# One operation and one transpose for the statistics' rows of two token tiles

## The chip, the core and the metric

The kernel runs on one core of a Trainium2 chip. The core has five engines that run at the same time and wait for each other through semaphores: PE (TensorE, matrix products), DVE (VectorE), ACT (ScalarE), POOL (GpSimd) and SP (which here only issues loads and stores). Each engine takes its instructions strictly in the order in which the program gives them. Operands lie in SBUF; PE writes to PSUM, which has eight banks here, each holding one 128x512 tile of fp32.

The metric is the device time of one execution in microseconds (us). For the kernel before the change the median of three runs is 441.87 us (440.46 to 442.1). The profiled execution, from which every duration below is taken, took 440.71 us; the span between its first and last instruction is 439.0 us.

## The reference

The block is a linear-attention block followed by a token-mixing MLP, both with a layer norm modulated by vectors that come from `c`. Sizes: 2048 tokens (S), 448 channels (D), 16 heads of 28, 1792 hidden features.

```python
x = A_x
mod = (_silu(c) @ w_mod).reshape(c.shape[0], 6, 1, -1)
sa, ca, ga, sb, cb, gb = (mod[:, 0], mod[:, 1], mod[:, 2], mod[:, 3], mod[:, 4], mod[:, 5])
h = _layernorm(x, axis=-1) * (1 + ca) + sa
x = x + ga * _A_ref(h, A_wqkv, A_wo)
h = _layernorm(x, axis=-1) * (1 + cb) + sb
x = x + gb * _B_ref(h, B_w1, B_b1, B_w2, B_b2)

def _A_ref(x, wqkv, wo):
    qkv = (x @ wqkv).reshape(B, S, 3, H, Dh).transpose(2, 0, 3, 1, 4)
    phi = lambda t: jnp.where(t > 0, t + 1, jnp.exp(t)) + 1e-6
    pq, pk = phi(q), phi(k)
    kv = jnp.einsum("bhsd,bhse->bhde", pk, v)
    z = jnp.einsum("bhsd->bhd", pk)
    num = jnp.einsum("bhqd,bhde->bhqe", pq, kv)
    den = jnp.einsum("bhqd,bhd->bhq", pq, z)[..., None] + 1e-6
    return (num / den).transpose(0, 2, 1, 3).reshape(B, S, D) @ wo
```

The change concerns the first layer norm alone: the mean and the standard deviation of each token over its 448 channels.

## The kernel before, in words

The tokens are cut into 16 tiles of 128. Every product is made with three single-pass products of a number cut into a high part (rounded) and a low part (the rest): high by high, high by low, low by high. In names, `hh` and `hl` are the high and low parts of a transposed token tile, `pkh` and `pkl` those of phi(k), `xh` and `xl` those of the normalized tile, `wh` and `wl` those of the weights.

The work runs in three stages. The first, up to about 101 us, makes phi(k) of all token tiles and sums the outer product of phi(k) with the normalized tiles in four PSUM banks (`cacc`). The second, to about 234 us, makes the attention output, the second layer norm and the first products of the MLP. The third makes the rest of the MLP. The change lies in the first stage only.

In the first stage the layer norm is not applied ahead of the projection. `project` (L428) multiplies the raw token tile by the weights in ten matmuls into a bank `kp`; `close` (L432) adds one more matmul, which multiplies four rows of statistics by four rows that were summed from the weights; and `a_exp` (L438) applies the reciprocal standard deviation as the scale of the exponential. The four rows of one tile are the mean and the standard deviation, each in a high and a low part. They come about in this way:

- `a_stats_dve` (L368): VectorE makes mean and variance of a tile (`bn_stats` into `st`, `bn_aggr` into `mv`), adds epsilon (`ve`), and GpSimd raises that to the powers 0.5 and -0.5 (`a_pow`, L348), so that `mv` holds mean, standard deviation and its reciprocal. Tiles 0 to 3 are done on ScalarE instead, tiles 4 and 5 as a pair, and from tile 6 on one tile at a time (`a_stats`).
- `a_rows` (L386): VectorE writes mean and standard deviation into columns of a 128x128 tile `rowst`, first the high parts (a CAST, which rounds), then the low parts (a subtraction, L391). `RING` such tiles are used in turn.
- `a_transpose` (L395): PE turns `rowst` into a PSUM bank `rw`.
- `a_copy` (L401): ScalarE copies 34 rows of the bank into a free corner of the tile's `hl`, where `close` reads them.

The order of the work is written out by hand: each engine's queue is the order of the calls in the code. After a start-up part, steps t = 4 to 15 of a loop (L628) do in this order: `project` of tile t+1, `close` of tile t, `a_transpose` of tile t+1, the outer product `a_outer` of tile t-4 (11 matmuls), from step 10 on also a projection to q (`a_q`, bank `qp`), then the rows of tile t+2, the statistics of tile t+3, ScalarE's copy of the transposed rows of tile t+1, `a_exp` of tile t, and the cuts of the tiles t+3, t-1 and t-2 into parts.

PSUM banks come from one pool of eight (`bank`). Four of them are `cacc` for the whole stage, so `kp`, `rw`, `qp` and a few others take turns in the other four: the first matmul into a bank waits until the reader of what stood there is done.

Of the kernel before, what the change touches and what calls it, by code (L numbers as in the profile page):

```python
# [14 lines left out]
P = 128  # L15
S, D, F = 2048, 448, 1792
NT = S // P
# [33 lines left out]
def block_kernel(ctx: ExitStack, tc: tile.TileContext, x, xt, wqkv, wo, w1, b1, w2, b2, c, wmod, wfirst, out):  # L51
# [276 lines left out]
            done["split"] += 1  # L328


    heads, mv, xn = {}, {}, {}
    junk = slot("junk")

    def b_square(src, nm, acc, name):
# [15 lines left out]
    def a_stats_act(ts):  # L350
        n = len(ts)
        g, ve = a_group(ts)
        sm = small.tile([P, n, 3], F32, name=f"as{ts[0]}", tag=f"as{n}")

        def one(i):
            t, s3 = ts[i], sm[:, i, :]
            nc.scalar.activation(junk, X[t], AF.Identity, accum_out=s3[:, 0:1])
            nc.scalar.activation(s3[:, 1:2], s3[:, 0:1], AF.Copy, scale=-1.0 / D)
            b_square(X[t], s3[:, 1:2], s3[:, 2:3], f"s{t}")

        def end():
# [3 lines left out]
            a_pow(g, ve)  # L365
        return one, end

    def a_stats_dve(ts):  # L368
        g, ve = a_group(ts)

        def one(i):
            b6 = small.tile([P, 6], F32, name=f"st{ts[i]}", tag="st")
            nc.vector.bn_stats(b6, X[ts[i]])
            nc.vector.bn_aggr(mv[ts[i]][:, 0:2], b6)

        def end():
            nc.vector.tensor_scalar_add(ve, g[:, :, 1:2].to_broadcast([P, len(ts), 2]), EPS)  # L377
            a_pow(g, ve)
        return one, end

    def a_stats(t):
        one, end = a_stats_dve((t,))
        one(0)
        end()

    def a_rows(t):  # L386
        r = rowst[t % RING]
        pair = mv[t][:, 0:2]
        nc.vector.tensor_copy(r[:, 64:].rearrange("p (b c) -> p b c", b=2)[:, :, 0:2],
                              pair.unsqueeze(1).to_broadcast([P, 2, 2]))  # L390
        nc.vector.tensor_sub(r[:, 66:68], pair, r[:, 64:66].bitcast(F32))  # L391

    tps = {}

    def a_transpose(t0, n=1):  # L395
        ps = bank(f"rw{t0}")
        for i in range(n):
            tps[t0 + i] = ps[:, i * P:(i + 1) * P]
            nc.tensor.transpose(tps[t0 + i][:ROWS], rowst[(t0 + i) % RING][:, :ROWS].bitcast(F32), ident)

    def a_copy(t):  # L401
        nc.scalar.activation(heads[t][1][64:ROWS, 384:], tps.pop(t)[64:ROWS], AF.Copy)

    def a_split_high(t):
        heads[t] = (slot(f"hh{t}", 512, F32R), slot(f"hl{t}", 512, F32R))
# [115 lines left out]
    def a_outer(t):  # L521
        if not cacc:
            cacc.extend(bank(f"cacc{ch}") for ch in range(4))
        xh, xl = xss.pop(t)
        kh, kl = pks.pop(t)
        for ch in range(4):
            s = slice(ch * P, (ch + 1) * P)
            todo = [(xh, kh), (xh, kl)] + ([(xl, kh)] if ch < 3 else [])
            for i, (a, b) in enumerate(todo):
                nc.tensor.matmul(cacc[ch][:, :D], a[:, s], b, start=(t == 0 and i == 0),  # L530
                                 stop=(t == NT - 1 and i == len(todo) - 1))

    pc = bank("col1")
    for k in range(2):
# [26 lines left out]
    col_out(0, pc)  # L561
    for ch in range(4):
        row_part(1, ch)
    a_rows(0)
    a_rows(1)
    project(3, 1, "kp")
    a_transpose(0, 2)
    row_bias(1)
    a_split(4)
    a_norm(0)  # L570
    dve45, end45 = a_stats_dve((4, 5))
    dve45(0)
    act23, end23 = a_stats_act((2, 3))
    act23(0)
    act23(1)
    end23()
    a_copy(0)
    a_copy(1)
    row_out(1)
    a_rows(2)  # L580
    a_rows(3)
    a_high(0)
    load_xt(9)
    load_x(9)
# [4 lines left out]
    a_split(5)  # L589
    a_low(0)  # L590
    kps = [close(t, 1) for t in (0, 1)]
    a_transpose(2, 2)
    project(5, 1, "kp")
    a_exp(0, kps[0])
    a_pk(0, kps[0])
    dve45(1)
    end45()
    a_copy(2)
    a_copy(3)
# [3 lines left out]
    a_pk_parts(0)  # L603
    a_outer(0)
    a_pk(1, kps[1])
    a_rows(4)
    a_rows(5)
    a_transpose(4, 2)
    a_exp(2, kps[2])
    a_split_high(6)  # L610
    a_pk(2, kps[2])
# [16 lines left out]
    for t in range(4, NT):  # L628
        if 5 < t < NT - 1:
            project(t + 1, 1, "kp")  # L630
        kp = close(t, 1) if t > 4 else kps[4]
        if 4 < t < NT - 1:
            a_transpose(t + 1)
        if t == 9:
            row_sum(0)
            row_bias(0)
        if t > 4:
            a_outer(t - KV_LAG)
        if t in Q_EARLY:
            a_q(Q_EARLY[t])  # L640
        if t == 12:
            mp = mod_sum2(2)
        if 4 < t < NT - 2:
            a_rows(t + 2)
        if 5 <= t < 9:
            w_low(0, t - 5)
            row_part(0, t - 5)
        if 7 < t + 3 < NT:
            a_stats(t + 3)
        a_phi_q(t in Q_EARLY)  # L650
        if 4 < t < NT - 1:
            a_copy(t + 1)
        a_exp(t, kp)
        if t + 3 < NT:
            a_split_high(t + 3)
# [2 lines left out]
        for i in highs[:1]:  # L658
            a_norm(i)
            a_high(i)  # L660
        a_pk(t, kp)
        if t + 3 < NT:
            a_split_low(t + 3)
        for i in highs[1:]:
# [622 lines left out]
```

## Time and profile before

| | busy | share of the span |
|---|---|---|
| span of the profiled execution | 439.0 us (the execution: 440.71 us) | |
| PE matmul | 433.3 us | 99% |
| DVE | 364.0 us | 83% |
| ACT | 279.4 us | 64% |
| POOL | 118.2 us | 27% |

The part that the change touches, by stretches of the same profile (us of busy time in each):

| stretch, us | PE | DVE | ACT | POOL |
|---|---|---|---|---|
| 20 to 37 (17.0) | 16.13 | 15.50 | 15.65 | 6.60 |
| 37 to 57 (20.0) | 19.95 | 19.52 | 18.61 | 11.92 |
| 57 to 101 (44.0) | 44.00 | 34.97 | 29.05 | 13.37 |
| 101 to 234 (133.0) | 133.00 | 114.67 | 99.36 | 54.46 |

A row of the timeline view, which is used most below, has the start in us from the span's start, the duration in us, the engine, the line of the code, the operation, `out<-in` by the tiles' names, shapes, a count of merged instructions, and in brackets the idle time of the engine before it with what ended it. Matmuls overlap: one is shown for about 0.36 us, but the next one starts about 0.20 us after it. Time that PE loses is therefore read from the distance of two starts, not from the idle time alone.

### The profile page before, as it was taken

To read this page: it belongs to the slowest core of one execution; us is meant where nothing else is said; L and a number is where in the kernel's file an instruction comes from. 1 tells how busy PE (TensorE), PEld (TensorE's weight loads), DVE (VectorE), ACT (ScalarE), POOL (GpSimd) and SP (SyncE) were. 2 spreads that over 40 slices of the span, in tenths; PEclk is the share of its full clock that TensorE was granted. 3 is DMA by queue.
4 is the path that set the end of the run, shared out by engine and by line. 5 is a ranking of instruction groups with operands and counts; after the bars stand their busy time and mean duration, and the time that the engine had idled before them with its cause. 6 is when DMAs were issued, how large, how long until landed. Compare 5 with 4: busy or idle time off the path is not lost.

```text
span 439.0 us, 7315 instructions
## 1 busy us (share of the span) xinstructions
PE 433.3 (99%) x2383; PEld 401.3 (91%) x2383; DVE 364.0 (83%) x822; ACT 279.4 (64%) x598; POOL 118.2 (27%) x200
## 2 busy tenths in 40 slices
PE   8999999999999999999999999999999999999996
PEld 7878899999899999999999999999999999999996
DVE  3989998689889999995579785829799988898894
ACT  3899877657676698885765263627555555655550
POOL 3137554300004567783300000010112231132010
PEclk9999999999999999999999999999999999999999
DMA  7997999545410025534616661579379987985430
GB/s 244 385 311 162 220 227 246 95 140 187 127 30 1 24 50 135 105 74 96 193 61 199 204 189 45 145 206 234 59 182 229 193 183 156 225 171 125 85 52 32
DMA packets 64085, 66.17 MB, mean 151 GB/s; under 512 B 4976, under 2 KB 55600, under 8 KB 64048
## 3 DMA queue, kind: packets, MB, share of 16 engines
q1 hardware_dynamic: 55120, 51.17, 38.3%
q0 software_dynamic: 8928, 14.55, 21.0%
q8 instruction: 18, 0.29, 0.3%
q14 instruction: 19, 0.16, 0.1%
HBM read 46.11 MB, written 7.34 MB: 122 GB/s over the span
## 4 chain that ended last, share of the span: by engine, by line
PE 96%; DVE 1%; ACT 1%; issue 0%; ACTq 0%
PE y L1077 19%; PE up L860 10%; PE up L861 10%; PE up L862 10%; PE y L1078 9%; PE op L810 8%; PE cacc L530 8%; PE qp L426 7%; PE kp L426 6%; PE tq L785 1%; PE col L218 1%; PE warm L181 1%; PE qp L433 1%; PE kvb L741 1%; PE rowb L283 1%; PE wp L877 1%
## 5 line engine op out<-in xcount | busy, mean ns | idle before, releaser
L860 PE MATMUL up<-h2h,ph 128*128 128x448 f32 x224 | 81.3, 363 | 0.0
L862 PE MATMUL up<-h2h,pl 128*128 128x448 f32 x224 | 81.1, 362 | 0.0
L861 PE MATMUL up<-h2l,ph 128*128 128x448 f32 x224 | 80.9, 361 | 0.0
L1032 POOL DMA_DIRECT2D a<-a x16 | 14.2, 963 | 139.4 <-DMA pr<-in_B_w_dram 75.3
L862 PEld LDWEIGHTS up<-h2h,pl 128*128 128x128 f32 x224 | 42.0, 188 | 3.1
L861 PEld LDWEIGHTS up<-h2l,ph 128*128 128x128 f32 x224 | 41.9, 187 | 3.1 <-DVE h2l L857 0.3
L860 PEld LDWEIGHTS up<-h2h,ph 128*128 128x128 f32 x224 | 42.0, 188 | 2.5
L83 DVE TENSOR_TENSOR pl<-pr,ph 128x512 fp32r<-128x512 f32 x46 | 30.8, 688 | 4.1 <-ACT ph L82 3.3
L1083 ACT ACTIVATE cc<-y 128x448 f32<-128x448 f32 x24 | 13.0, 546 | 26.8 <-PE y L1078 26.8
L82 ACT ACTIVATE ph<-pr 128x512 fp32r<-128x512 f32 x46 | 27.6, 624 | 0.8 <-PE up L862 0.5
L996 DVE TENSOR_TENSOR u<-u,mod 128x448 f32<-128x448 f32 x14 | 8.7, 623 | 21.6 <-ACT u L995 21.4
L530 PE MATMUL cacc<-pkh,xh 128*128 128x448 f32 x64 | 24.4, 382 | 0.3 <-ACT pkh L504 0.3
L810 PE MATMUL op<-wph,pth 128*128 128x448 f32 x64 | 24.5, 383 | 0.0
L995 ACT ACTIVATE u<-up,b1c 128x448 f32<-128x448 f32 x14 | 8.8, 625 | 24.1 <-PE up L862 23.5
L530 PE MATMUL cacc<-pkl,xh 128*128 128x448 f32 x64 | 23.3, 364 | 0.2 <-DVE pkl L506 0.2
L426 PE MATMUL kp<-wh,hh 128*128 128x448 f32 x64 | 23.2, 373 | 0.2 <-ACT wh L256 0.2
L426 PE MATMUL qp<-wh,hh 128*128 128x448 f32 x64 | 23.3, 364 | 0.0
L810 PE MATMUL op<-wpl,pth 128*128 128x448 f32 x64 | 23.1, 362 | 0.0
L1097 POOL DMA_DIRECT2D out_dram<-yt x14 | 12.5, 893 | 39.1 <-DVE yt L1088 29.7
L767 POOL TENSOR_SCALAR den<-den 128x16 f32<-128x16 f32 x16 | 8.8, 549 | 47.7 <-DVE den L764 47.7
L348 POOL TENSOR_TENSOR mv<-ve,roots 128x2 f32<-128x2 f32 (+1 forms) x13 | 12.5, 960 | 22.4 <-DVE ve L377 21.6
L1038 DVE TENSOR_TENSOR a<-a,s 128x512 f32<-128x512 f32 (+1 forms) x32 | 18.5, 619 | 0.0
(238 smaller groups left out, 1382.7 us busy)
## 6 DMA issues: line engine op xcount, KB each, us to landing
pr<-in_B_w_dram SPq DMA_DIRECT2D x56, 256.0 KB, 3.3
a<-in_B_w_dram SPq DMA_DIRECT2D x32, 256.0 KB, 4.8
a<-in_B_w_dram SPq DMA_DIRECT2D x32, 192.0 KB, 4.6
xt<-in_xt_dram SPq DMA_DIRECT2D x16, 256.0 KB, 4.9
x<-in_A_x_dram SPq DMA_DIRECT2D x16, 224.0 KB, 4.8
wm<-in_B_wmod_dram SPq DMA_DIRECT2D x16, 196.0 KB, 4.8
out_dram<-x SPq DMA_DIRECT2D x14, 224.0 KB, 2.2
out_dram<-yt POOLq DMA_DIRECT2D x14, 224.0 KB, 6.3
```

The source lines that it names most:

```text
L82: nc.scalar.activation(hi, full, AF.Copy)
L83: nc.vector.tensor_sub(lo, full, hi.bitcast(F32))
L426: nc.tensor.matmul(pps[t, j][:, :D], a[:, ch * P:(ch + 1) * P], w, start=first, stop=False)
L530: nc.tensor.matmul(cacc[ch][:, :D], a[:, s], b, start=(t == 0 and i == 0), stop=(t == NT - 1 and i == len(todo) - 1))
L810: nc.tensor.matmul(opb[t][:, :D], a, b, start=(n == 0), stop=(n == len(todo) - 1))
L860: nc.tensor.matmul(ps[:, :D], hi[:, sl], mh, start=first, stop=False)
L861: nc.tensor.matmul(ps[:, :D], hi[:, sl], ml, start=False, stop=False)
L862: nc.tensor.matmul(ps[:, :D], lo[:, sl], mh, start=False, stop=last)
L1032: nc.gpsimd.dma_start(w, a, accum_op=ALU.add)
L1038: nc.vector.tensor_tensor(w, raw2[q, a][i], raw2[q, b][i], op=op)
L1077: nc.tensor.matmul(ps[:, :D], h[:, s], w, start=opens and r == 0, stop=False, skip_group_check=True)
L1078: nc.tensor.matmul(ps[:, :HD], l[:, s], wh, start=False, stop=closes and r == PAIRS - 1, skip_group_check=True)
```

## The change

The rows of two neighbouring tiles are made together. `rowst` now has room for two tiles, 64 columns each, and the ring has three of them instead of six. One CAST writes the high parts of both tiles, one subtraction the low parts of both, one transpose turns both, and the two copies read rows 0 to 33 and 64 to 97 of the same bank. From tile 6 on the statistics are finished for pairs too: one `ve` and one power for two tiles.

With that the calls move. In the loop, odd steps t = 5 to 13 transpose the tiles t+1 and t+2, behind the outer product of the step and no longer ahead of it, and ScalarE copies both at that step. The rows of the pair (t+2, t+3) are made at even steps t = 4 to 12. Operations on VectorE that use each other's results are set apart where other work stands near: `first` (`bn_stats`) and `second` (`bn_aggr`) have the weights' low part between them, `end` (`ve`) stands ahead of the row sum, and the CAST of the rows and the subtraction have phi(k) of the step between them. Statistics of tile 7 come ahead of the low parts of phi(k) and of the normalized tile of tile 1.

In `a_outer` the matmuls of the first two tiles that read `pkl`, phi(k)'s low part, come last, after the seven others of the tile.

```diff
-RING = 6
+RING = 3
...
     def a_stats_dve(ts):
         g, ve = a_group(ts)
 
-        def one(i):
-            b6 = small.tile([P, 6], F32, name=f"st{ts[i]}", tag="st")
-            nc.vector.bn_stats(b6, X[ts[i]])
-            nc.vector.bn_aggr(mv[ts[i]][:, 0:2], b6)
+        b6 = {}
+
+        def first(i):
+            b6[i] = small.tile([P, 6], F32, name=f"st{ts[i]}", tag="st")
+            nc.vector.bn_stats(b6[i], X[ts[i]])
+
+        def second(i):
+            nc.vector.bn_aggr(mv[ts[i]][:, 0:2], b6[i])
 
         def end():
             nc.vector.tensor_scalar_add(ve, g[:, :, 1:2].to_broadcast([P, len(ts), 2]), EPS)
             a_pow(g, ve)
...
     def a_rows(t):
-        r = rowst[t % RING]
-        pair = mv[t][:, 0:2]
-        nc.vector.tensor_copy(r[:, 64:].rearrange("p (b c) -> p b c", b=2)[:, :, 0:2],
-                              pair.unsqueeze(1).to_broadcast([P, 2, 2]))
-        nc.vector.tensor_sub(r[:, 66:68], pair, r[:, 64:66].bitcast(F32))
-
-    tps = {}
-
-    def a_transpose(t0, n=1):
-        ps = bank(f"rw{t0}")
-        for i in range(n):
-            tps[t0 + i] = ps[:, i * P:(i + 1) * P]
-            nc.tensor.transpose(tps[t0 + i][:ROWS], rowst[(t0 + i) % RING][:, :ROWS].bitcast(F32), ident)
+        g, r = groups.pop(t)[:, :, 0:2], rowst[t // 2 % RING].rearrange("p (t b c) -> p t b c", t=2, b=2)
+        nc.vector.tensor_copy(r[:, :, :, 0:2], g.unsqueeze(2).to_broadcast([P, 2, 2, 2]))
+
+        def low():
+            nc.vector.tensor_sub(r[:, :, 0, 2:4], g, r[:, :, 0, 0:2].bitcast(F32))
+        return low
+
+    def a_transpose(t):
+        ps = bank(f"rw{t}")
+        tps[t], tps[t + 1] = ps[:ROWS - 64, :P], ps[64:ROWS, :P]
+        nc.tensor.transpose(ps[:ROWS, :P], rowst[t // 2 % RING][:, :ROWS].bitcast(F32), ident)
 
     def a_copy(t):
-        nc.scalar.activation(heads[t][1][64:ROWS, 384:], tps.pop(t)[64:ROWS], AF.Copy)
+        nc.scalar.activation(heads[t][1][64:ROWS, 384:], tps.pop(t), AF.Copy)
...
         for ch in range(4):
             s = slice(ch * P, (ch + 1) * P)
             todo = [(xh, kh), (xh, kl)] + ([(xl, kh)] if ch < 3 else [])
-            for i, (a, b) in enumerate(todo):
+            for i, (a, b) in enumerate(todo[::1 if t > 1 else 2]):
                 nc.tensor.matmul(cacc[ch][:, :D], a[:, s], b, start=(t == 0 and i == 0),
                                  stop=(t == NT - 1 and i == len(todo) - 1))
+        if t < 2:
+            for ch in range(4):
+                nc.tensor.matmul(cacc[ch][:, :D], xh[:, ch * P:(ch + 1) * P], kl, start=False, stop=False)
...
-    a_stats(6)
+    first, second, end = a_stats_dve((6, 7))
+    first(0)
+    first(1)
+    second(0)
+    second(1)
+    end()
     a_pk_parts(1)
     a_low(1)
-    a_rows(6)
     a_pk(3, kps[3])
     a_pk_parts(2)
-    a_stats(7)
...
         kp = close(t, 1) if t > 4 else kps[4]
-        if 4 < t < NT - 1:
-            a_transpose(t + 1)
         if t == 9:
             row_sum(0)
             row_bias(0)
         if t > 4:
             a_outer(t - KV_LAG)
+        if t % 2 and 4 < t < NT - 2:
+            a_transpose(t + 1)
...
-        if 4 < t < NT - 2:
-            a_rows(t + 2)
+        if 7 < t + 3 < NT:
+            if t % 2:
+                first, second, end = a_stats_dve((t + 3, t + 4))
+            first(1 - t % 2)
+            if t % 2 == 0:
+                second(1)
         if 5 <= t < 9:
             w_low(0, t - 5)
+        if 7 < t + 3 < NT:
+            second(0) if t % 2 else end()
+        if 5 <= t < 9:
             row_part(0, t - 5)
-        if 7 < t + 3 < NT:
-            a_stats(t + 3)
         a_phi_q(t in Q_EARLY)
-        if 4 < t < NT - 1:
+        if t % 2 and 4 < t < NT - 2:
             a_copy(t + 1)
+            a_copy(t + 2)
         a_exp(t, kp)
...
+        if t % 2 == 0 and t < NT - 3:
+            low = a_rows(t + 2)
         a_pk(t, kp)
+        if t % 2 == 0 and t < NT - 3:
+            low()
```

What stands in the engines' queues is shown at three places. Numbers after a tile's name tell buffers apart; the line numbers of the two codes differ by one to five.

The first is PE, the outer product of tile 0 (`cacc`), followed by the transpose of the rows of tiles 4 and 5 (`rw4`) and the projection of tile 6. Before:

```order
L530 MATMUL cacc0_465<-pkh0_461,xh0_388 128x448
L530 MATMUL cacc0_465<-pkl0_462,xh0_388 128x448
L530 MATMUL cacc0_465<-pkh0_461,xl0_389 128x448
L530 MATMUL cacc1_466<-pkh0_461,xh0_388 128x448
L530 MATMUL cacc1_466<-pkl0_462,xh0_388 128x448
L530 MATMUL cacc1_466<-pkh0_461,xl0_389 128x448
```

Now, from the same place on:

```order
L531 MATMUL cacc0_453<-pkh0_449,xh0_377 128x448
L531 MATMUL cacc0_453<-pkh0_449,xl0_378 128x448
L531 MATMUL cacc1_454<-pkh0_449,xh0_377 128x448
L531 MATMUL cacc1_454<-pkh0_449,xl0_378 128x448
L531 MATMUL cacc2_455<-pkh0_449,xh0_377 128x448
L531 MATMUL cacc2_455<-pkh0_449,xl0_378 128x448
L531 MATMUL cacc3_456<-pkh0_449,xh0_377 128x448
L535 MATMUL cacc0_453<-pkl0_450,xh0_377 128x448
```

The matmul that reads `pkl0` was the second of the tile and is now the eighth.

The second is PE at the end of step 9 and the start of step 10: the end of the outer product of tile 5, and the projection of tile 11 (`kp11`). Before, where the transpose `rw10` stood further ahead, after the `close` of tile 9 and ahead of the row sum and of this outer product:

```order
L530 MATMUL cacc2_467<-pkh5_681,xh5_752 128x448
L530 MATMUL cacc2_467<-pkl5_682,xh5_752 128x448
L530 MATMUL cacc2_467<-pkh5_681,xl5_753 128x448
L530 MATMUL cacc3_468<-pkh5_681,xh5_752 128x448
L530 MATMUL cacc3_468<-pkl5_682,xh5_752 128x448
L426 MATMUL kp11_927<-wh1_0_238,hh11_819 128x448
L426 MATMUL kp11_927<-wl1_0_240,hh11_819 128x448
```

Now:

```order
L531 MATMUL cacc2_455<-pkh5_652,xh5_722 128x448
L531 MATMUL cacc2_455<-pkl5_653,xh5_722 128x448
L531 MATMUL cacc2_455<-pkh5_652,xl5_723 128x448
L531 MATMUL cacc3_456<-pkh5_652,xh5_722 128x448
L531 MATMUL cacc3_456<-pkl5_653,xh5_722 128x448
L400 MATMUL rw10_848<-ident_78,rowst2_108 98x128
L427 MATMUL kp11_889<-wh1_0_232,hh11_782 128x448
L427 MATMUL kp11_889<-wl1_0_234,hh11_782 128x448
```

In both programs `kp11` takes the PSUM bank that held `rw10`, so its first matmul waits until ScalarE has copied the rows out of it. The transpose, which stood far ahead, now stands right ahead of that matmul.

The third is VectorE at step 6, from the low part of the normalized tile 3 to the low part of token tile 9. Before:

```order
L494 TENSOR_TENSOR xl3_623<-xn3_620,xh3_622 128x384
L389 CAST rowst2_108<-mv8_599 128x2x2
L391 TENSOR_TENSOR rowst2_108<-mv8_599,rowst2_108 128x2
L268 SCALAR_TENSOR_TENSOR wl0_1_663<-wr0_1_168,col1_233,wh0_1_630 128x448
L276 SCALAR_TENSOR_TENSOR accb0_597<-wr0_1_168,col0_329,accb0_597 128x448
L373 BN_STATS st9_668<-x9_393 128x6
L374 BN_AGGR mv9_666<-st9_668 128x2
L377 TENSOR_SCALAR ve9_667<-mv9_666 128x2
L484 TENSOR_SCALAR xn4_687<-x4_160,mv4_363 128x448
L446 SCALAR_TENSOR_TENSOR pk6_692<-ek6_674,rk6_675 128x448
L409 TENSOR_TENSOR hl9_679<-xt9_391,hh9_678 128x512
```

Now:

```order
L495 TENSOR_TENSOR xl3_601<-xn3_598,xh3_600 128x384
L376 BN_STATS st9_637<-x9_382 128x6
L379 BN_AGGR mv8_574<-st9_637 128x2
L268 SCALAR_TENSOR_TENSOR wl0_1_640<-wr0_1_162,col1_227,wh0_1_608 128x448
L382 TENSOR_SCALAR ve8_575<-mv8_574 128x4
L276 SCALAR_TENSOR_TENSOR accb0_581<-wr0_1_162,col0_323,accb0_581 128x448
L485 TENSOR_SCALAR xn4_658<-x4_154,mv4_354 128x448
L391 CAST rowst1_106<-mv8_574 128x4x2
L447 SCALAR_TENSOR_TENSOR pk6_664<-ek6_645,rk6_646 128x448
L394 TENSOR_TENSOR rowst1_106<-mv8_574,rowst1_106 128x2x2
L410 TENSOR_TENSOR hl9_650<-xt9_380,hh9_649 128x512
```

The CAST now needs the power that GpSimd makes of the `ve` three rows above it, in the same step; before, the one that it needed was made from a `ve` of the step before. The CAST and its subtraction have moved from ahead of the weights' low part to both sides of `pk6`, so `hl9` still stands behind all of them.

More of the change, by code (lines that the diff above doesn't have):

```diff
@@ L328, in split_to @@
             done["split"] += 1
-    heads, mv, xn = {}, {}, {}
+    heads, mv, xn, groups = {}, {}, {}, {}
     junk = slot("junk")
@@ L365, in end @@
             a_pow(g, ve)
+            groups[ts[0]] = g
         return one, end
@@ L378, in end @@
             a_pow(g, ve)
[L379 to L384, printed above, removed]
[L386 to L399 removed]
+            groups[ts[0]] = g
+        return first, second, end
+    tps = {}
+    def a_rows(t):
+        g, r = groups.pop(t)[:, :, 0:2], rowst[t // 2 % RING].rearrange("p (t b c) -> p t b c", t=2, b=2)
[7 more added lines that the diff above has]
+        nc.tensor.transpose(ps[:ROWS, :P], rowst[t // 2 % RING][:, :ROWS].bitcast(F32), ident)
     def a_copy(t):
[L402 removed]
+        nc.scalar.activation(heads[t][1][64:ROWS, 384:], tps.pop(t), AF.Copy)
     def a_split_high(t):
```

26 lines of the change are left out of this document (14 added, 12 removed).

## The prediction

> **What bounds the kernel now.** I read the page first (busy times, the chain that ended last), then TensorE's timeline in the first stage, because the change touches nothing else, and then the other engines' rows at the places where TensorE stands still.
>
> ```profile
> span 439.0 us, 7315 instructions
> PE 433.3 (99%) x2383; PEld 401.3 (91%) x2383; DVE 364.0 (83%) x822; ACT 279.4 (64%) x598; POOL 118.2 (27%) x200
> ...
> PE 96%; DVE 1%; ACT 1%; issue 0%; ACTq 0%
> ```
>
> TensorE is the bound: it holds 96% of the chain that ended last. So I ask two things: which TensorE time goes, and which waits of TensorE go or come. Busy time hides these waits, since matmuls overlap; the starts show them.
>
> ```profile
> 25.35 0.36 PE L426 MATMUL kp<-wl,hh 128*128 128x448 f32 x1
> 25.68 0.47 PE L426 MATMUL kp<-wh,hl 128*128 128x448 f32 x1
> ...
> 27.39 0.57 PE L433 MATMUL kp<-wrow,hl 98*128 98x448 f32 x2
> 28.31 0.47 PE L530 MATMUL cacc<-pkh,xh 128*128 128x448 f32 x1 [0.34 <-ACT pkh L504]
> 28.97 0.47 PE L530 MATMUL cacc<-pkl,xh 128*128 128x448 f32 x1 [0.19 <-DVE pkl L506]
> 29.27 0.37 PE L530 MATMUL cacc<-pkh,xl 128*128 128x448 f32 x1
> ...
> 31.22 0.45 PE L426 MATMUL kp<-wh,hh 128*128 128x448 f32 x1
> ...
> 33.31 0.58 PE L433 MATMUL kp<-wrow,hl 98*128 98x448 f32 x2
> 34.23 0.29 PE L399 MATMUL rw<-ident,rowst 128*98 128x128 f32 x1 [0.34 <-DVE rowst L391]
> ...
> 36.77 0.37 PE L426 MATMUL kp<-wl,hh 128*128 128x448 f32 x1
> 37.18 0.47 PE L426 MATMUL kp<-wh,hl 128*128 128x448 f32 x1
> ```
>
> A matmul of this size is followed after 0.20 us when nothing is in the way; one that has waited is followed after 0.30 (28.97 to 29.27). These steps are too long: 25.35 to 25.68 (0.13, and 0.10 behind it); two matmuls from 27.39, good for 0.40, and then 28.31 (0.52); 28.31 to 28.97 (0.46, and 0.10 behind it); two matmuls from 33.31 and then 34.23 (0.52); 36.77 to 37.18 (0.21, and 0.10). Together 2.1 us. Later in the stage I find no such step. What the change is worth lies in these waits, in the transposes, and in waits that come new.
>
> **What a transpose costs.** Here is one between its neighbours:
>
> ```profile
> 39.09 0.27 PE L399 MATMUL rw<-ident,rowst 128*98 128x128 f32 x1
> 39.12 0.45 PE L530 MATMUL cacc<-pkh,xh 128*128 128x448 f32 x1
> 39.41 0.36 PE L530 MATMUL cacc<-pkl,xh 128*128 128x448 f32 x1
> ```
>
> From 39.09 to 39.41 are 0.32 us for a transpose and one matmul; the matmul alone takes 0.20. So a transpose costs 0.12 us, although it is shown with 0.27. Eight of sixteen go, 0.96 us in all. Three of them fall ahead of 35 us, between waits, and are counted there. Five (tiles 7, 9, 11, 13, 15) fall where TensorE is full: **0.6 us gained**.
>
> **The part from 21 to 38 us.** The rows of VectorE and of ScalarE that set it:
>
> ```profile
> 29.36 0.16 DVE L389 CAST rowst<-mv 128x4 fp32r<-128x4 f32 x1
> 29.56 0.16 DVE L391 TENSOR_TENSOR rowst<-mv,rowst 128x2 fp32r<-128x2 f32 x1
> 29.64 0.16 DVE L389 CAST rowst<-mv 128x4 fp32r<-128x4 f32 x1
> ...
> 31.05 0.62 DVE L373 BATCH_NORM_STATS2 st<-x 128x6 f32<-128x448 f32 x1
> 31.71 0.18 DVE L374 BATCH_NORM_AGGREGATE mv<-st 128x2 f32<-128x6 f32 x1
> 31.92 0.17 DVE L377 TENSOR_SCALAR ve<-mv 128x2 f32<-128x2 f32 x1
> 32.57 0.63 DVE L506 SCALAR_TENSOR_TENSOR pkl<-pk,pkh 128x448 fp32r<-128x448 f32 x1 [0.48 <-ACT pkh L504]
> ...
> 33.25 0.55 DVE L494 TENSOR_TENSOR xl<-xn,xh 128x384 fp32r<-128x384 f32 x1
> ...
> 36.44 0.68 DVE L409 TENSOR_TENSOR hl<-xt,hh 128x512 fp32r<-128x512 f32 x1
> ```
>
> ```profile
> 30.22 0.66 ACT L441 ACTIVATE rk<-kp,mv 128x448 f32<-128x448 f32 x1
> 30.73 0.61 ACT L488 ACTIVATE xh<-xn 128x448 fp32r<-128x448 f32 x1
> 31.50 0.44 ACT L402 ACTIVATE hl<-rw 34x128 fp32r<-34x128 f32 x2 [0.16 <-PE rw L399]
> ...
> 33.77 0.63 ACT L440 ACTIVATE ek<-kp,mv 128x448 f32<-128x448 f32 x1 [0.16 <-PE kp L433]
> ```
>
> A CAST and its subtraction take 29.64 - 29.36 = 0.28 us of VectorE: 0.20 until the subtraction may start, 0.08 until the next, independent operation. An operation that must wait for the one ahead of it thus costs 0.12 more. `bn_stats` (0.66 to the next) would take 0.54 without that, and `bn_stats`, `bn_aggr`, `ve` together take 0.66 + 0.21 + 0.09 = 0.95.
>
> The 21 VectorE instructions that go (8 CASTs, 8 subtractions, 5 `ve`) take 8 x 0.28 + 5 x 0.09 = 2.7 us by these rows. If all of it reached TensorE in place of the 1.0 us found below, the sum would be -2.0 us. The Trainium skill, page "Perfetto Trace Analysis", section "Optimizing Scalar/DVE Operations", puts the overhead of a VectorE operation on SBUF at about 60 ns and says that grouping helps where the engine is saturated; by that the 21 instructions are an estimated 1.3 us and the sum would be -0.6. The rows of small operations are dearer than the page's figure. I take neither whole, since TensorE gets only what it waits for:
>
> 1. The first wait, for `hl` of tile 5, stays. One transpose less ahead of `close` of tile 0 moves ScalarE's chain forward by 0.11, so the outer product of tile 0 starts at 28.20 instead of 28.31.
> 2. The wait for `pkl` goes: seven matmuls, about 1.5 us, now stand ahead of its first use, where 0.66 would do. That is 0.46 more, and one transpose less is 0.12: TensorE reaches tile 6's projection 0.69 earlier, at 30.53. There the bank is tile 3's until its `rk` ends, 30.88 - 0.11 = 30.77. So 30.82: 0.40 earlier.
> 3. The wait for `rowst` goes from its place: the outer product of tile 1 follows `close` of tile 5 directly, at 33.31 + 0.40 - 0.40 = 33.31. Its second matmul needs `xl` of tile 1. VectorE starts tile 6's statistics 0.28 + 0.11 earlier, at 30.66, does tile 7's too (30.66 + 0.54 + 0.54 + 0.10 + 0.21 + 0.09 = 32.14), and waits for `pkh` of tile 1. ScalarE makes its copies when `xh` is done, at 31.25 and not at 31.50, so `pkl` comes at 32.57 - 0.25 = 32.32 and `xl` at 33.00 to 33.55. TensorE loses 0.1 to 0.2 there and ends the eleven matmuls at 35.75.
> 4. From `xl` to the end of tile 7's `hl` VectorE needs 37.12 - 33.25 = 3.87 now; 0.95 goes (tile 7's statistics are done) and 0.12 (CAST and subtraction are apart): 33.00 + 2.80 = 35.80, with the rows ready before it. The transpose at 35.75 and the projection's third matmul at 36.27 wait for nothing.
>
> That matmul stands at 37.18 now, with 0.10 behind it: **1.0 us gained**. Bounds: 0.5, if `hl` of tile 7 keeps half of its delay; 1.5, if all waits from 27 us on go.
>
> **Two waits that come.** TensorE is now earlier, and its suppliers less so.
>
> ```profile
> 27.84 1.20 POOL L348 TENSOR_TENSOR mv<-ve,roots 128x4 f32<-128x4 f32 x1 [4.16 <-DVE ve L377]
> ```
>
> ```profile
> 40.55 0.56 ACT L488 ACTIVATE xh<-xn 128x448 fp32r<-128x448 f32 x1
> ...
> 41.41 0.22 DVE L493 TENSOR_TENSOR xh<-xn,xh 128x64 fp32r<-128x64 f32 x1
> ...
> 45.39 0.68 DVE L409 TENSOR_TENSOR hl<-xt,hh 128x512 fp32r<-128x512 f32 x1
> ...
> 46.33 0.36 PE L426 MATMUL kp<-wh,hl 128*128 128x448 f32 x1
> ```
>
> Tile 9's `hl` ends at 46.07 and TensorE takes it at 46.33: 0.26 us of margin. TensorE will be there 1.0 + 0.12 earlier, at 45.21. VectorE's stretch up to it begins with `xh` of tile 3, which it cannot begin before ScalarE's part. ScalarE is 0.41 earlier (0.25, and its wait of 0.16 at 33.77) less 0.22 for the second copy, now made at step 5 (half of the x2 row): its part ends at 41.11 - 0.19 = 40.92, and VectorE starts at 40.96, not 41.41. The stretch holds the same operations, two dependent pairs less (-0.24). But the CAST waits for GpSimd's power, 1.20 for a pair, plus `ve`'s own 0.17, and two operations of about 0.54 cover it: +0.2. So 40.96 + 4.66 - 0.24 + 0.2 = 45.58 against 45.21, and 0.10 behind a wait: **0.5 us lost**. Ends: nothing, if ScalarE comes half a microsecond earlier; 0.9, if it comes no earlier at all.
>
> ```profile
> 55.38 0.27 ACT L402 ACTIVATE hl<-rw 34x128 fp32r<-34x128 f32 x1
> ```
>
> ```profile
> 57.24 0.36 PE L426 MATMUL kp<-wh,hh 128*128 128x448 f32 x1
> ```
>
> At step 9 the transpose of tiles 10 and 11 now stands right ahead of tile 11's projection, the matmul at 57.24, which takes its bank. With 0.7 us of gain left by then it comes at about 56.5; ScalarE was at this step's copy at 55.38, so it stands ready. From the transpose's start: 0.27 for itself, 0.04 until ScalarE starts, 0.44 for both copies, 0.05 to the matmul, where 0.03 would do: **0.8 us lost**. Ends: 0.4, if the copies overlap more; 1.1, if ScalarE is 0.3 late.
>
> The Trainium skill, page "Perfetto Trace Analysis", section "Matmuls", speaks against such a place: independent groups of matmuls should rotate through PSUM banks, so that the evacuation of one overlaps the next group. The rows agree for step 9 alone: after step 5 and step 7 the next projection goes to another bank, and after steps 11 and 13 the eleven matmuls of `a_q`, 2.2 us, stand between.
>
> The other edits cost nothing on TensorE's path. The copies wait for the transposes at steps 9, 11 and 13 and make ScalarE up to 2 us late, but the parts of phi(k) that follow are used four steps later. To 101 us and beyond the others follow TensorE, as this stretch shows, so what is gained early is kept:
>
> ```profile
> 57.00:101.00 44.00, 44.00 (x224) 40.86 (x223) 34.97 (x86) 29.05 (x57) 13.37 (x15) 1.00 0.76 181
> ```
>
> **The sum.** -1.0 - 0.6 + 0.5 + 0.8 = -0.3 us against the profiled 440.71 us, and the same against the median 441.87, which is 0.26% above it: 441.6 us. The runs spread from 440.46 to 442.1; 0.5%, 2.2 us, is about what a measurement can tell from no change.
>
> **Rivals.** *Neither new wait comes:* -1.6 us, 440.3. For it: ScalarE's lead is an estimate in tenths. Against it: the bank of step 9 is fixed by the program. *All waits of the stage go:* 2.1 + 0.96 = 3.1 us, 438.8, faster. Against it: the first two hang on ScalarE's chain, which moves by 0.11. *GpSimd's power comes late, slower:* VectorE now waits for GpSimd within a step, and `hl` behind it waits too. GpSimd also issues transfers, and an issue can stand:
>
> ```profile
> 44.60 0.91 POOL L348 TENSOR_TENSOR mv<-ve,roots 128x2 f32<-128x2 f32 x1 [1.80 <-DVE ve L377]
> ...
> 62.26 0.88 POOL L513 DMA_DIRECT2D pk<-pk  x1 [1.75 <-issue]
> ```
>
> If the power of tiles 8 and 9 falls behind such an issue, 1.75 + 0.88 = 2.6 us go straight to tile 9's `hl`: +2.3, 444.2. It decides from about 0.3 us on, where the gain is used up. Against it: ahead of that power GpSimd has idled for 1.80. *Every transposed pair costs its copies:* five times 0.8 in place of one, +2.9, 444.8; the banks and `a_q` speak against it. The rule on rotating banks in the Trainium skill, page "Perfetto Trace Analysis", section "Matmuls", would give this if it held at every pair.
>
> **Chances.** Forecast 0.60; neither wait 0.16; all waits gone 0.07; late power 0.11; copies everywhere 0.06. The last two are slower by over 0.5% (0.17), the third faster (0.07), the rest within (0.76). The forecast's own bounds, -0.6 with -1.5 to -0.5, 0 to 0.9 and 0.4 to 1.1, reach from -1.7 to +0.9, or 440.2 to 442.8. Half of the 1.6 by which the runs lie apart puts the lower end at 439.5; the upper end goes on to the late power, 444.2, so that all waits gone and copies everywhere (0.13) and the tails are left out.
>
> **What would show it.** Right: no wait of `cacc` for `pkl` near 28 us; eight `rw` matmuls; a wait of the projection for ScalarE's copy of about 0.8 us near 56 us and none like it elsewhere; a wait for `hl` near 45 us. Wrong: waits of VectorE for `mv` of over 1 us, or one more wait of TensorE in steps 11 to 14.

## The result, and the profile after

The changed kernel takes 443.38 us (median of 6 runs, 442.74 to 444.84); the kernel before takes 440.52 us (6 runs, 440.15 to 442.1). The ratio is 1.0059, with a 95% interval from 1.0036 to 1.0082: the change makes it slower by 0.6%. The forecast, 441.6 us and probably no measurable change, was wrong; its range, 439.5 to 444.2, holds the time. A ratio here is not the quotient of the two medians and can differ from it by about 0.1%; where they differ, the ratio with its interval decides.

The head of the changed kernel's page, and its chain that ended last:

```profile
span 441.9 us, 7277 instructions
PE 435.0 (98%) x2375; PEld 401.0 (91%) x2375; DVE 360.9 (82%) x801; ACT 278.4 (63%) x598; POOL 113.4 (26%) x192
...
PE 96%; DMA 1%; ACT 1%; DVE 1%; SPq 0%; issue 0%; ACTq 0%
```

TensorE still holds 96% of the chain. It does eight transposes less and is busy 1.7 us longer; VectorE is busy 3.1 us less, and the time does not show it. To see where the time went I compare three points of TensorE's timeline: the first projection (`kp`), the first attention output (`op`), which comes after everything that the change touches, and the first product of the last stage (`y`). Before:

```profile
10.72 0.48 PE L426 MATMUL kp<-wh,hh 128*128 128x448 f32 x1 [0.22 <-ACT wh L256]
...
124.23 0.45 PE L810 MATMUL op<-wph,pth 128*128 128x448 f32 x1
...
311.92 0.36 PE L1077 MATMUL y<-ub,a11h 128*128 128x448 f32 x1
```

After:

```profile
11.24 0.47 PE L427 MATMUL kp<-wh,hh 128*128 128x448 f32 x1 [0.27 <-ACT wh L256]
...
126.14 0.46 PE L829 MATMUL op<-wph,pth 128*128 128x448 f32 x1
...
315.06 0.37 PE L1096 MATMUL y<-ub,a11h 128*128 128x448 f32 x1
```

The first projection starts 0.52 us later. That is scatter of this execution, the slowest of the six: in the other twelve profiles of this study, six of variants of the changed kernel among them, it starts between 10.07 and 10.75. ScalarE's first operation on a token tile waits for its transfer until 7.66 us before and 8.50 after. From there to `op` are 113.5 us before and 114.9 after (+1.4), from `op` to `y` 187.7 and 188.9 (+1.2), and from `y` to the end of the last matmul 123.65 and 123.35 (-0.3). So 1.2 us are lost between 126 and 315 us, where the change edits nothing.

The waits of TensorE that the prediction spoke of, after:

```profile
27.64 0.57 PE L434 MATMUL kp<-wrow,hl 98*128 98x448 f32 x2
29.00 0.47 PE L531 MATMUL cacc<-pkh,xh 128*128 128x448 f32 x1 [0.78 <-ACT pkh L505]
29.30 0.36 PE L531 MATMUL cacc<-pkh,xl 128*128 128x448 f32 x1
...
45.49 0.37 PE L531 MATMUL cacc<-pkl,xh 128*128 128x448 f32 x1
46.43 0.32 PE L400 MATMUL rw<-ident,rowst 128*98 128x128 f32 x1 [0.57 <-DVE rowst L394]
...
57.79 0.27 PE L400 MATMUL rw<-ident,rowst 128*98 128x128 f32 x1
58.71 0.47 PE L427 MATMUL kp<-wh,hh 128*128 128x448 f32 x1 [0.66 <-ACT hl L403]
```

The wait for `pkl` is gone. Two waits are new, at the two steps where they were forecast: 45.49 to 46.43 (0.73 over a normal step), and 57.79 to 58.71, where the projection of tile 11 waits for ScalarE's copies out of its bank. They explain the waiting part, but not the rest. That shows only where nothing waits. Eleven full-width matmuls of one query projection, from the first of them to the first matmul behind, before:

```profile
61.77 0.36 PE L426 MATMUL qp<-wh,hh 128*128 128x448 f32 x1
...
63.98 0.37 PE L426 MATMUL kp<-wh,hh 128*128 128x448 f32 x1
```

and after:

```profile
63.27 0.37 PE L427 MATMUL qp<-wh,hh 128*128 128x448 f32 x1
...
65.54 0.37 PE L427 MATMUL kp<-wh,hh 128*128 128x448 f32 x1
```

2.21 us became 2.27 for the same eleven matmuls. Over the whole trace I take the distances of the starts of neighbouring matmuls, those between 185 and 225 ns (steps of full width that wait for nothing). Their mean by what the matmul makes, in ns:

| | kp | qp | op | cacc | up |
|---|---|---|---|---|---|
| before | 201.0 | 201.0 | 200.6 | 200.3 | 200.1 |
| after | 205.3 | 206.1 | 204.6 | 200.4 | 200.4 |

With 166, 173 and 161 such steps, `kp` loses 0.7 us, `qp` 0.9 and `op` 0.65: 2.2 us. The outer products `cacc` lose nothing. What `kp`, `qp` and `op` share is the pool of their wide operand (the one with 448 columns, `wh`, `wl`, `wrow`, `wph`, `wpl`): the weights' pool. The wide operand of `cacc` and `up` lies in the slots' pool.

### The profile page after: what moved, and what is told of

The parts are those of the page before. It is cut to its first block, busy times and chain, and to the rows that moved or that the text cites. A ratio compares the mean times of both kernels' runs of the same rounds, so it can differ in the third digit from the quotient of the medians.

```text
span 441.9 us, 7277 instructions
## 1 busy us (share of the span) xinstructions
PE 435.0 (98%) x2375; PEld 401.0 (91%) x2375; DVE 360.9 (82%) x801; ACT 278.4 (63%) x598; POOL 113.4 (26%) x192
## 4 chain that ended last, share of the span: by engine, by line
PE 96%; DMA 1%; ACT 1%; DVE 1%; SPq 0%; issue 0%; ACTq 0%
PE y L1096 18%; PE up L879 10%; PE up L881 10%; PE up L880 10%; PE y L1097 9%; PE op L829 8%; PE cacc L531 8%; PE qp L427 7%; PE kp L427 7%; DMA xt<-in_xt_dram 1%; PE tq L804 1%; PE qp L434 1%; PE kvb L760 1%; PE wp L896 1%; PE rowb L283 1%; PE kp L434 1%
## 5 line engine op out<-in xcount | busy, mean ns | idle before, releaser
L531 PE MATMUL cacc<-pkl,xh 128*128 128x448 f32 x56 | 20.3, 363 | 0.0
L1096 PE MATMUL y<-ut,s1h 128*128 128x448 f32 x56 | 18.1, 374 | 0.0
```

Source lines behind the costliest of these rows:

```text
L1096: nc.tensor.matmul(ps[:, :D], h[:, s], w, start=opens and r == 0, stop=False, skip_group_check=True)
```

## Where the weights lie

The built programs say where each tile lies. The weights' pool stands behind the constants, and the constants and the pool of small tiles ahead of them became smaller: three `rowst` tiles less (3 x 512 bytes), the `ve` tiles for a single token tile (128 bytes), and eight `mv` tiles in place of thirteen, each with 32 bytes (160 bytes). Together 1824 bytes, which is 28 x 64 + 32. A wide operand begins 64 bytes into its tile (`moving` cuts columns from 16 on). The operand of one weight tile (a `wh` of the projection to q) began at byte 200896 of its partition, which leaves 64 when divided by 128; it now begins at 199072, which leaves 32. The tiles of the pool lie a multiple of 2048 bytes apart, so the remainder is the same for all of them. The slots lie ahead of the constants and did not move. The 32 come from the five `mv` tiles alone; the rest is a multiple of 64.

The theory is then: TensorE takes a full-width matmul every 201 ns when its wide operand begins at remainder 64, and every 205 to 206 at remainder 32. Rivals: the new order of the work, or transfers that meet the reads.

## Experiments on the address

There is an unused tile `space` in the constants. Its size moves all that lies behind it.

```diff
-    cst.tile([P, 40], F32, name="space")
+    cst.tile([P, 48], F32, name="space")     # the changed kernel, +32 bytes
```

> The changed kernel with 32 bytes more in the unused tile that stands in the constant pool, so that the weights and the constants behind it move up by 32 bytes; nothing else. Theory A (the weights' address): the projections' full-width matmuls kp, qp and op go back from 205.3, 206.1 and 204.6 ns apart to about 201, which is 0.7 + 0.9 + 0.65 = 2.2 us; the time comes to about 441.0, within 0.2% of the kernel before, and the two waits of TensorE near 45 and 58 us stay. Theory B (the order of the work made it slower): nothing moves, 443.4. Theory C (the weights are read while more transfers write to the memory): nothing moves, 443.4.

Measured: 441.35 us against 441.07 for the kernel before, ratio 1.0006 (0.9995 to 1.0017). The 0.6% are gone.

```diff
-    cst.tile([P, 40], F32, name="space")
+    cst.tile([P, 32], F32, name="space")     # the kernel before, -32 bytes
```

> The kernel before with 32 bytes less in the same unused tile, so that the weights lie 32 bytes off as in the changed kernel; its order of work is untouched. Theory A: kp, qp and op go to 205 to 206 ns apart, 2.0 to 2.4 us more, about 442.7, and no new wait comes. Theories B and C: no change, 440.5.

Measured: 443.6 against 441.07, ratio 1.0056 (1.0042 to 1.0071): the kernel before becomes as slow as the changed one by 32 bytes alone.

```diff
-    cst.tile([P, 40], F32, name="space")
+    cst.tile([P, 24], F32, name="space")     # the kernel before, -64 bytes
```

> The kernel before with 64 bytes less there: the first weight that a matmul reads then lies on a multiple of 128 bytes, where it lies 64 behind one now. Theory A, if what counts is the remainder by 64: no change, 440.5. If what counts is the remainder by 128, with 64 the good one: the pitch rises to more than 201 ns, by an unknown size (the y matmuls, whose operands lie on such a multiple in part, stand 212 apart). Theories B and C: no change.

Measured: 441.95, ratio 1.0022 (1.0013 to 1.0031). The remainder by 64 is the same and it is still slower, so 64 is not the whole of it.

```diff
-    cst.tile([P, 40], F32, name="space")
+    cst.tile([P, 56], F32, name="space")     # the changed kernel, +64 bytes
```

> The changed kernel with 64 bytes more there: the remainder by 64 stays what it is (32), so that it is a control for the first run. Theory A by 64: no change against the changed kernel, kp, qp, op near 205 ns, 443.4. Theory A by 128: another pitch than 205. If instead any shift helps, it falls to 441.

Measured: 444.1, ratio 1.0072 (1.0057 to 1.0087). A shift as such helps nothing.

The same eleven matmuls as above (first `qp`, first `kp` behind it) in the four kernels, in this order: the changed one with 32 bytes more,

```profile
62.44 0.36 PE L427 MATMUL qp<-wh,hh 128*128 128x448 f32 x1
...
64.64 0.36 PE L427 MATMUL kp<-wh,hh 128*128 128x448 f32 x1
```

the one before with 32 less,

```profile
61.81 0.36 PE L426 MATMUL qp<-wh,hh 128*128 128x448 f32 x1
...
64.08 0.37 PE L426 MATMUL kp<-wh,hh 128*128 128x448 f32 x1
```

the one before with 64 less,

```profile
61.42 0.36 PE L426 MATMUL qp<-wh,hh 128*128 128x448 f32 x1
...
63.66 0.37 PE L426 MATMUL kp<-wh,hh 128*128 128x448 f32 x1
```

and the changed one with 64 more:

```profile
62.44 0.37 PE L427 MATMUL qp<-wh,hh 128*128 128x448 f32 x1
...
64.69 0.36 PE L427 MATMUL kp<-wh,hh 128*128 128x448 f32 x1
```

2.20, 2.27, 2.24 and 2.25 us. So the order of the work is out as the cause, and transfers too: the first two kernels differ from their originals by an address alone.

Two more runs ask whether it is the wide operand itself, and not something else behind `space`. In both, `space` is as before, and only some operands begin at column 24 of their tiles:

```diff
-    def moving(new, name, dt=F32R, parts=P):
-        return new(name, dt=dt, parts=parts, w=512)[:, 16:16 + D]
+    def moving(new, name, dt=F32R, parts=P, at=16):
+        return new(name, dt=dt, parts=parts, w=512)[:, at:at + D]
...
-        hi = moving(tslot, f"wph{ch}")
+        hi = moving(tslot, f"wph{ch}", at=24)
...
-        Wpl.append(moving(tslot, f"wpl{ch}"))
+        Wpl.append(moving(tslot, f"wpl{ch}", at=24))
```

> The kernel before; only the two halves of the attention's output weights (wph, wpl) begin 24 instead of 16 numbers into their tiles, 32 bytes further. If the address of the matmul's wide operand is what counts: op alone goes from 200.6 to about 205 ns apart (161 full-width steps, 0.7 us), kp and qp stay at 201.0; about 441.7 against 441.05. If the shift acted through something else that lies behind the unused tile: no change.

Measured: 441.64 against 441.17, ratio 1.0015 (1.0005 to 1.0025), which is 0.66 us. `op` goes to 204.9 ns, `kp` and `qp` stay at 201. Here is one token tile's output product, from its first matmul to the `qp` behind its eleven; at this place both kernels happen to start at the same time. Before, then with the shifted weights:

```profile
133.93 0.45 PE L810 MATMUL op<-wph,pth 128*128 128x448 f32 x1
...
136.22 0.36 PE L426 MATMUL qp<-wh,hh 128*128 128x448 f32 x1
```

```profile
133.93 0.45 PE L810 MATMUL op<-wph,pth 128*128 128x448 f32 x1
...
136.26 0.37 PE L426 MATMUL qp<-wh,hh 128*128 128x448 f32 x1
```

The other run does the same to the wide operand of the outer products, in the other pool:

```diff
-        hi, lo = moving(slot, f"pkh{t}"), moving(slot, f"pkl{t}")
+        hi, lo = moving(slot, f"pkh{t}", at=24), moving(slot, f"pkl{t}", at=24)
```

> The kernel before; only the two parts of phi(k) (pkh, pkl), which are the wide operand of the outer products, begin 32 bytes further. These tiles lie in another pool. If the address of the wide operand counts: cacc goes from 200.3 to about 205 ns apart (164 full-width steps, 0.8 us), kp, qp and op stay. If it is a property of the weights' pool: no change.

Measured: `cacc` goes from 200.3 to 205.3 ns, and the others stay. That is 0.8 us in the steps; the time is 441.34 against 441.17, ratio 1.0006 (0.9993 to 1.0019), no difference that can be told. From the first projection to the first `op` its trace is 0.5 us longer, so some 0.3 of the 0.8 did not reach `op`. That it ended in waits that stood there anyway is likely, but not shown.

All eight kernels in one table, by the remainder at which the operand begins (by 128):

| | remainder of the weights | kp | qp | op | cacc |
|---|---|---|---|---|---|
| before | 64 | 201.0 | 201.0 | 200.6 | 200.3 |
| changed, +32 bytes | 64 | 200.8 | 200.9 | 200.0 | 200.5 |
| changed | 32 | 205.3 | 206.1 | 204.6 | 200.4 |
| before, -32 bytes | 32 | 205.7 | 205.8 | 204.5 | 200.1 |
| changed, +64 bytes | 96 | 205.3 | 205.4 | 205.4 | 200.9 |
| before, -64 bytes | 0 | 203.3 | 204.7 | 203.8 | 200.2 |
| before, `op` weights at 96 | 64, `op` 96 | 201.2 | 201.0 | 204.9 | 200.3 |
| before, phi(k) at 96 | 64, phi(k) 96 | 200.6 | 201.0 | 200.5 | 205.3 |

Every group that begins at 64 stands at 200 to 201 ns, every other one at 203 to 206. That the pattern repeats every 128 bytes is not shown: divided by 256, every operand in the rows and columns at 64 leaves 192 (200896 does, and so does phi(k)'s), and no run put an operand of these groups at 64 by 256.

## Experiments on the order of the work

The run with 32 bytes more is the changed kernel without the address effect, and its first projection starts at 10.68, 0.04 from the kernel before. So the prediction's steps can be read in it directly. Its two new waits on TensorE:

```profile
44.63 0.36 PE L531 MATMUL cacc<-pkl,xh 128*128 128x448 f32 x1
45.64 0.32 PE L400 MATMUL rw<-ident,rowst 128*98 128x128 f32 x1 [0.65 <-DVE rowst L394]
...
56.99 0.27 PE L400 MATMUL rw<-ident,rowst 128*98 128x128 f32 x1
57.91 0.47 PE L427 MATMUL kp<-wh,hh 128*128 128x448 f32 x1 [0.65 <-ACT hl L403]
```

and on VectorE, ahead of the first of them:

```profile
44.80 0.17 DVE L391 CAST rowst<-mv 128x8 fp32r<-128x8 f32 x1 [0.51 <-POOL mv L348]
```

The transpose of tiles 8 and 9 waits for their rows, and VectorE's CAST waits 0.51 us for GpSimd's power. Three runs take these waits away, on top of the 32 bytes. What a single edit is worth is read from one trace each; the times of the first two cannot be told from those of the kernel before. First the power earlier:

```diff
             if t % 2 == 0:
                 second(1)
+                end()
         if 5 <= t < 9:
             w_low(0, t - 5)
-        if 7 < t + 3 < NT:
-            second(0) if t % 2 else end()
+        if t % 2 and 7 < t + 3 < NT:
+            second(0)
```

> The kernel of e1_after_p32 (changed kernel, weights back on their remainder), and in the even steps the eps addition and GpSimd's power of the pair directly behind the second aggregation, ahead of the weights' low part. Theory (VectorE's CAST waits for GpSimd's power, and TensorE's transpose of tiles 8 and 9 waits for the rows): the CAST's idle time of 0.51 us near 44.8 us goes, the rows of tiles 8 and 9 are ready at about 45.1 instead of 45.6, and TensorE's step of 1.01 us ahead of that transpose shrinks to 0.5; the time falls by 0.5, to about 440.8. Rival (VectorE has no time there, and the wait moves to the low part of tile 9): the transpose comes earlier, but the projection waits instead; under 0.2 us gained.

TensorE's rows:

```profile
44.39 0.37 PE L531 MATMUL cacc<-pkl,xh 128*128 128x448 f32 x1
45.13 0.32 PE L400 MATMUL rw<-ident,rowst 128*98 128x128 f32 x1 [0.37 <-DVE rowst L394]
```

and VectorE's:

```profile
43.71 0.51 DVE L485 TENSOR_SCALAR xn<-x,mv 128x448 f32<-128x448 f32 x1
44.29 0.17 DVE L391 CAST rowst<-mv 128x8 fp32r<-128x8 f32 x1
```

The CAST no longer stands idle for GpSimd, and TensorE's step falls from 1.01 to 0.74 us: about half of what was expected, between theory and rival. Measured against its own first projection, VectorE reaches `xn`, ahead of the CAST, 0.2 us later than without the edit. From the first projection to the first `op` the trace is 0.24 us shorter (113.61 against 113.85). The time is 440.81, ratio 1.0004 (0.9994 to 1.0014) to the kernel before.

Second, the transpose at step 9 in the middle of the outer product:

```diff
-            a_outer(t - KV_LAG)
-        if t % 2 and 4 < t < NT - 2:
+            a_outer(t - KV_LAG, (lambda: a_transpose(10)) if t == 9 else None)
+        if t % 2 and 4 < t < NT - 2 and t != 9:
             a_transpose(t + 1)
...
-    def a_outer(t):
+    def a_outer(t, mid=None):
...
         for ch in range(4):
             s = slice(ch * P, (ch + 1) * P)
+            if ch == 2 and mid:
+                mid()
```

> The kernel of e1_after_p32, and at step 9 the transpose of tiles 10 and 11 stands in the middle of the outer product (behind its second channel) instead of behind it. Theory (the projection of tile 11 waits for ScalarE's copies out of its bank): the step of 0.92 us near 57 us goes, 0.7 to 0.8 gained, about 440.6. Rival (the rows of tiles 10 and 11 come only at 55.1, or ScalarE is late): the wait moves into the outer product, under 0.2 gained.

```profile
55.80 0.36 PE L533 MATMUL cacc<-pkh,xl 128*128 128x448 f32 x1
56.00 0.27 PE L400 MATMUL rw<-ident,rowst 128*98 128x128 f32 x1
...
56.92 0.36 PE L533 MATMUL cacc<-pkl,xh 128*128 128x448 f32 x1
57.12 0.37 PE L427 MATMUL kp<-wh,hh 128*128 128x448 f32 x1
```

The transpose waits for nothing, and the projection follows after 0.20. The trace is 0.95 us shorter up to `op` (112.90); the time is 440.75, ratio 0.9993 (0.9981 to 1.0006). The Trainium skill, page "Perfetto Trace Analysis", section "Matmuls", asks for groups that rotate through PSUM banks so that an evacuation overlaps the next group's matmuls. The trace agrees for this step, at 0.95 us; the transposes at steps 11 and 13, which have `a_q` behind them, stand without a wait in every profile of the changed kernel and its variants.

Third, both edits:

> Both edits on e1_after_p32. If the two waits are separate: 1.2 to 1.3 us gained, about 440.1, 0.2% under the kernel before. If the time that TensorE gains near 45 us is lost again at the next supplier (low part of tile 10, or xl): about 440.6.

Measured: 439.82 against 441.03, ratio 0.9985 (0.9972 to 0.9997); one of its eleven executions took 1520.37 us, for a reason that is not known, and the ratio is made without it. Up to `op` its trace takes 112.71 us, 1.14 less than without them and 0.8 less than the kernel before. The two gains, 0.24 and 0.95, add up; this is the one kernel of the study that is faster than both.

Two runs look at the low parts last. Alone, in the kernel before:

```diff
-            for i, (a, b) in enumerate(todo):
+            for i, (a, b) in enumerate(todo[::1 if t > 1 else 2]):
                 nc.tensor.matmul(cacc[ch][:, :D], a[:, s], b, start=(t == 0 and i == 0),
                                  stop=(t == NT - 1 and i == len(todo) - 1))
+        if t < 2:
+            for ch in range(4):
+                nc.tensor.matmul(cacc[ch][:, :D], xh[:, ch * P:(ch + 1) * P], kl, start=False, stop=False)
```

> The kernel before with only the low parts last in the first two outer products. The step of 0.66 us ahead of the first product with pkl (28.31 to 28.97) becomes 0.30. If the bank and the rows of tiles 6 and 7 set the pace behind it (the prediction's step 2 and 3): TensorE is 0.4 earlier at 31 us and waits as much longer for rowst near 34 us, so that nothing is gained, 441.1. Rival: the 0.4 us is kept, 440.7.

```profile
28.29 0.47 PE L530 MATMUL cacc<-pkh,xh 128*128 128x448 f32 x1 [0.33 <-ACT pkh L504]
28.60 0.36 PE L530 MATMUL cacc<-pkh,xl 128*128 128x448 f32 x1
...
34.07 0.29 PE L399 MATMUL rw<-ident,rowst 128*98 128x128 f32 x1 [0.46 <-DVE rowst L391]
```

The wait for `pkl` is gone, and the one for `rowst` ends at 34.07 in place of 34.23. Of the 0.4 in question, 0.16 is kept there and 0.24 up to `op` (113.26 against 113.50): between theory and rival. The time is 440.61, ratio 0.9998 (0.9988 to 1.0009). And undone, in the changed kernel with 32 bytes more:

```diff
-            for i, (a, b) in enumerate(todo[::1 if t > 1 else 2]):
+            for i, (a, b) in enumerate(todo):
...
-        if t < 2:
-            for ch in range(4):
-                nc.tensor.matmul(cacc[ch][:, :D], xh[:, ch * P:(ch + 1) * P], kl, start=False, stop=False)
```

> The kernel of e1_after_p32 with the old order in the first two outer products, so that pkl is used by the second matmul. If the wait for the rows of tiles 8 and 9 near 45 us takes back what TensorE gained before it: a step of 0.6 to 0.7 us for pkl comes near 28.5 us, TensorE is up to 0.4 later until 44 us, the step ahead of that transpose shrinks from 1.01 by as much, and behind 48 us nothing has changed against e1 (within 0.1). If the early gain is kept: everything behind is 0.4 later.

```profile
27.61 0.47 PE L531 MATMUL cacc<-pkh,xh 128*128 128x448 f32 x1 [0.65 <-ACT pkh L505]
28.27 0.47 PE L531 MATMUL cacc<-pkl,xh 128*128 128x448 f32 x1 [0.19 <-DVE pkl L507]
...
44.01 0.37 PE L531 MATMUL cacc<-pkl,xh 128*128 128x448 f32 x1
45.07 0.32 PE L400 MATMUL rw<-ident,rowst 128*98 128x128 f32 x1 [0.69 <-DVE rowst L394]
```

The step of 0.66 for `pkl` is back, and the first projection starts at 10.07 here, so 0.61 must be added for a comparison: the transpose comes at 45.68, against 45.64. Up to `op` it is 113.90 against 113.85. The total is as expected, the way is not: TensorE is only 0.2 later at tile 6's projection, and 0.1 earlier at tile 7's, because the wait of 0.20 for `xl` in the second outer product, with 0.10 behind it, falls away. The wait near 45 us does not shrink. In the changed kernel this edit is worth nothing by this trace. Its one timed execution took 440.38 us.

## Why the prediction was wrong

**The step that failed** is the sentence "The other edits cost nothing on TensorE's path". It went through the copies and the queues, and left out that a smaller ring and fewer `mv` tiles change where everything behind them lies in memory. The sum lacked one term, the address of the weights. By the traces (the changed kernel against itself with 32 bytes more) it is 1.06 us up to `op`, 1.27 from `op` to `y` and -0.30 behind: 2.0 us. By the ratios it is 0.59% less 0.06%, 2.3 us. The cost of the address is shown by the runs above; why the memory or TensorE behaves so is open. The prediction looked at TensorE "in the first stage, because the change touches nothing else"; more than half of the loss lies behind that stage.

**The early part, forecast -1.0:** right, in the run without the address effect. The outer product of tile 0 was forecast at 28.20 and stands at 28.22, tile 6's projection at 30.82 and 30.84, the outer product of tile 1 at 33.31 and 33.36; tile 8's projection begins at 40.40 in place of 41.41, and 0.12 of this is tile 7's transpose. Only the share given to `pkl` was wrong: undoing it loses nothing, since `xl` or `rowst` takes its place.

**Transposes, forecast -0.6:** right in price. From tile 11's projection on, where three of the removed ones lie, the gap to the kernel before shrinks from +0.67 to +0.32 at 108 us, 0.12 for each. Tile 9's is kept too (between 48.17 and 54.43 TensorE goes from level to 0.25 ahead; about half of that is tile 10's transpose, which now stands behind that stretch); tile 7's stands ahead of the new wait and is lost in it.

**The wait for tile 9, forecast +0.5, ends 0 to 0.9:** the cause was right and the size wrong. TensorE is 1.03 us ahead at 42.61 and level with the kernel before at 48.17: 1.0 us, above the upper end. It waits at the transpose and not at `hl`, for the same chain. The forecast took ScalarE as 0.19 earlier and the wait for the power as 0.2; ScalarE's `xh` ends at 41.15 against 41.11 before, so its lead is gone, and the wait is 0.51. The power itself took longer than the 1.20 of the row that the forecast went by:

```profile
43.37 1.40 POOL L348 TENSOR_TENSOR mv<-ve,roots 128x4 f32<-128x4 f32 x1 [0.56 <-DVE ve L382]
```

**The bank at step 9, forecast +0.8, ends 0.4 to 1.1:** right. The step is 0.92, and without it 0.95 us are saved.

The sum without the address effect was forecast at -0.3; measured are +0.35 us up to `op` and +0.3 by the medians (ratio 1.0006). The wait for tile 9 (0.5 more) is nearly all of the difference, the bank (0.1 more) the rest.

**The rivals.** None of them is what happened. The late power, +2.3, would have given nearly the measured time, but it is there with 0.5 only. The range held the time for a reason that was not in it, which is luck. Two of the prediction's sums are slightly off, without effect on its argument: 0.66 + 0.21 + 0.09 is 0.96, and 440.2 less half of 1.6 is 439.4.

## What to carry to other kernels

When a change adds or removes tiles that live through the whole kernel, compare the addresses of the matmuls' wide operands in the two builds before costing anything else; 32 bytes were worth 2 us here, more than any edit of the order, and 32 bytes more in an unused tile undid them. The sign of it in a profile is a uniformly longer step between matmuls in code that was not edited; busy shares and waits do not show it. And a gain on the bounding engine lasts only until the next place where a supplier sets the time, so it must be followed to there.

## What was not expected of the hardware

- The distance of full-width matmuls depends on where the wide operand begins: 200 to 201 ns at remainder 64 by 128 bytes, 204.5 to 206 at 32 and 96, 203 to 205 at 0. It holds in two pools and for four groups of matmuls. Why 64 is best is open, and so is whether 128 is the right divisor. The Trainium skill, page "SBUF — State Buffer", section "Specifications (TRN2)", puts the memory's lines at 16 bytes; a contiguous operand that moves by 32 bytes keeps its place in such a line, so by that alone nothing would change. The runs show 4 to 5 ns for each matmul. The address is not the whole story either: in the changed kernel one projection, right behind the wait near 46 us, ran at 200 ns with its weights at remainder 32.
- The last stage, whose full-width matmuls alternate with half-width ones, does not follow this order: from the start of its first to the end of its last matmul it takes 123.65 us in all profiles where the pool of its wide operands that moves with the weights (`uparts`) is at remainder 64 (the one with the output weights shifted among them), 123.35 in the two at 32, 123.14 in the one at 0 and 124.14 in the one at 96. It was not looked into.
